# Holding a queue of loads back until an early tile has landed, in a kernel that TensorE fills

## The chip, the cores and the metric

One core of one Trainium2 chip. The metric is the time of one execution in device microseconds. Executions of this kernel differ from each other by up to 2 us, so a median of several is quoted, and most of this document is about that spread.

Engine names: PE is TensorE, PEld its weight loads, DVE VectorE, ACT ScalarE, POOL GpSimd, SP SyncE, which here issues most DMAs. "L232" is line 232 of the kernel.

## The reference

Layer norm of x (2048 x 512, bf16), then the sum of x, a linear-attention block and a gated feed-forward block:

```python
xn = layernorm(x)
# A: q, k, v = xn @ wqkv, 32 heads of 16; phi(t) = (t + 1 if t > 0 else exp(t)) + 1e-6
#    kv = sum_s phi(k)^T v ; z = sum_s phi(k) ; o = phi(q) kv / (phi(q) z + 1e-6) ; A = o @ wo
# B: (silu(xn @ w_gate) * (xn @ w_up)) @ w_down,   w_gate, w_up: 512 x 1792
out = x + A(xn) + B(xn)
```

## The kernel before

x is cut into 16 tiles of 128 rows (128 KB each, x0 to x15). For each tile VectorE makes the statistics (`bn1`, `bn2`), ScalarE the reciprocal deviation (`rs`), VectorE the scaled tile (`lna_dve`), TensorE transposes it (tiles 0 to 3) and projects it to K (`kproj`). `phi` of a K tile ends in a VectorE operation that writes `pk` and so frees the PSUM bank. The first Q projection (`qproj(0)`) needs the bank that the first K tile used, so it waits for that operation.

All engines run their own lists in the order in which they are written. The loads, in issue order on each queue:

```python
K.add("act", lambda e: e.preload_act_table_set("natural_log_exp_and_others"))
for h, eng in ((0, "sp"), (1, "act")):
    load(eng, ("x", 0, h), ...)        # x0 in two halves
xload("sp", 1)
xload("sp", 2)
wload("act", 1, 0, 2)                  # K weights, first half, 256 KB
xload("sp", 3)
wload("act", 1, 1, 2)                  # K weights, second half
wload("sp", 0)                         # Q weights, 512 KB
xload("act", 4)
xload("act", 5)
for t in range(6, 16):
    xload("sp", t)
```

The start of the program, which is the order that counts on VectorE:

```python
bn1(0); bn2(0); rs(0); bn1(1); lna_dve(0); transp(0, 0); keep_busy(NFILL, 256)
bn2(1); rs(1); evac(0, 0)
bn1(2); bn2(2); rs(2); lna_dve(1); transp(1, 1); evac(1, 1)
bn1(3); bn2(3); rs(3)                  # <- VectorE needs x3 here
k0 = kproj(0)
lna_dve(2); transp(2, 2); evac(2, 2, "dve")
k1 = kproj(1, late=True)
lna_dve(3); transp(3, 3); evac(3, 3)
k1 = k1()
norm(4)                                # <- bn1(4): x4
k2 = kproj(2); k3 = kproj(3)
stat(5)                                # <- bn1(5): x5, and only then:
k0()                                   # pk of tile 0, frees the bank
q0 = qproj(0)                          # the first Q matmul
# ... (cut) ...
```

`keep_busy(NFILL, 256)` issues filler matmuls on constants so that TensorE does not fall idle; NFILL is 3.

## Time and profile before

| | before |
|---|---|
| time, median of the first 3 runs | 216.06 us |
| time of the profiled execution | 216.84 us |
| its span | 215.1 us |
| PE busy | 209.6 us (97%) |
| first Q matmul in it | 12.37 us |
| x3 landed in it | 7.30 us |

From the page of the kernel before, the span and the first line of busy time and share:

```profile
span 215.1 us, 2648 instructions
PE 209.6 (97%) x996; PEld 96.7 (45%) x1015; DVE 102.1 (47%) x178; ACT 67.0 (31%) x132; POOL 41.3 (19%) x79
```

TensorE is the limit, so only time in which it stands idle can be won. The chain of waits, followed back from the end, tells where that is. These are its pieces in order of time; the columns are start in us, length in us, and what it was:

```profile
2.18 5.12 DMA x_sb<-in_A_x_dram
7.30 0.02 issue
7.32 0.70 DVE stats L232
8.05 0.18 DVE mv L235
8.23 0.31 DVE xn L245
...
10.94 0.59 DVE stats L232
...
11.74 0.59 DVE pk L295
12.32 0.05 issue
12.37 1.04 PE pb L312 x4
```

A load of x (x3, by its place) holds VectorE to 7.32. From there VectorE's list runs to `pk` and that releases the first Q matmul at 12.37. After that the pieces of the chain are PE, but for "issue" pieces of 0.05 us or less and VectorE's last output of 0.42 us. VectorE's own timeline shows the wait in brackets (start, length, engine, line, operation, operands, idle time before it and what ended it):

```profile
5.89 0.38 DVE L245 TENSOR_SCALAR xn<-x_sb,mv,rstd 128x512 bf16<-128x512 bf16 x1
7.32 0.69 DVE L232 BATCH_NORM_STATS2 stats<-x_sb 128x6 f32<-128x512 bf16 x1 [1.05 <-DMA x_sb<-in_A_x_dram]
```

Each load counts up its semaphore once for each of the 16 DMA engines. Of x3's sixteen counts fifteen had come by 6.16 us and the last came at 7.30 us.

### The profile page before, as it was taken

To read this page: it belongs to the slowest core of one execution; us is meant where nothing else is said; L and a number is where in the kernel's file an instruction comes from. 1 tells how busy PE (TensorE), PEld (TensorE's weight loads), DVE (VectorE), ACT (ScalarE), POOL (GpSimd) and SP (SyncE) were. 2 spreads that over 40 slices of the span, in tenths; PEclk is the share of its full clock that TensorE was granted. 3 is DMA by queue.
4 is the path that set the end of the run, shared out by engine and by line. 5 is a ranking of instruction groups with operands and counts; after the bars stand their busy time and mean duration, and the time that the engine had idled before them with its cause. 6 is when DMAs were issued, how large, how long until landed. Compare 5 with 4: busy or idle time off the path is not lost.

```text
span 215.1 us, 2648 instructions
## 1 busy us (share of the span) xinstructions
PE 209.6 (97%) x996; PEld 96.7 (45%) x1015; DVE 102.1 (47%) x178; ACT 67.0 (31%) x132; POOL 41.3 (19%) x79
## 2 busy tenths in 40 slices
PE   8799999999999999999999999999999999999995
PEld 3344444444544444444444444444444444444454
DVE  4699797556977633373433533222234423222121
ACT  3575665447363333321001333021123322110000
POOL 4164898999301100000000000000000000000000
PEclk9999999999999999999999999999999999999999
DMA  6923236999200399400000000000000000000001
GB/s 194 346 71 74 50 75 181 317 369 356 74 0 3 84 230 338 128 3 24 0 24 24 27 0 0 2 24 27 24 24 0 0 3 24 26 24 18 30 27 49
DMA packets 21725, 17.74 MB, mean 82 GB/s; under 512 B 7376, under 2 KB 21712, under 8 KB 21712
## 3 DMA queue, kind: packets, MB, share of 16 engines
q1 hardware_dynamic: 20736, 16.72, 26.1%
q10 hardware_dynamic: 976, 0.85, 1.3%
q8 instruction: 8, 0.13, 0.3%
q14 instruction: 5, 0.04, 0.1%
HBM read 11.80 MB, written 4.19 MB: 74 GB/s over the span
## 4 chain that ended last, share of the span: by engine, by line
PE 93%; DMA 2%; DVE 2%; issue 1%; SPq 1%
PE pb L444 45%; PE pb L547 22%; PE pb L312 6%; PE pb L543 6%; PE pb L319 6%; PE pb L301 5%; DMA x_sb<-in_A_x_dram 2%; DVE stats L232 1%; SPq L160 1%; PE pb L469 0%; PE pb L509 0%; DVE xn L245 0%; PE pb L494 0%; DVE pk L295 0%; DVE mv L235 0%
## 5 line engine op out<-in xcount | busy, mean ns | idle before, releaser
L452 ACT ACTIVATE sil<-pb 128x512 bf16<-128x512 f32 x56 | 33.3, 597 | 101.4 <-PE pb L444 100.2
L457 DVE TENSOR_TENSOR hT<-pb,sil 128x512 bf16<-128x512 f32 x56 | 38.5, 689 | 47.0 <-PE pb L444 46.3
L444 PE MATMUL pb<-xnT,wg 128*128 128x512 bf16 x217 | 57.0, 379 | 0.4
L444 PE MATMUL pb<-xnT,wu 128*128 128x512 bf16 x221 | 57.2, 379 | 0.1
L547 PE MATMUL pb<-wd,hT 128*128 128x512 bf16 (+1 forms) x234 | 50.9, 366 | 0.2
L547 PEld LDWEIGHTS pb<-wd,hT 128*128 128x128 bf16 x238 | 23.3, 98 | 25.1
L553 DVE TENSOR_TENSOR out_sb<-pb,x_sb 128x512 bf16<-128x512 f32 (+1 forms) x17 | 11.2, 660 | 47.2 <-PE pb L547 47.2
L444 PEld LDWEIGHTS pb<-xnT,wu 128*128 128x128 bf16 x224 | 21.9, 98 | 26.0
L444 PEld LDWEIGHTS pb<-xnT,wg 128*128 128x128 bf16 x224 | 21.7, 98 | 25.8 <-issue 0.4
L291 ACT ACTIVATE ef<-pb 128x512 bf16<-128x512 f32 x32 | 18.8, 593 | 10.9 <-PE pb L301 5.5
L292 POOL TENSOR_SCALAR ef<-ef 128x512 bf16<-128x512 bf16 x32 | 19.5, 616 | 11.9 <-ACT ef L291 11.5
L543 PE MATMUL pb<-M,pqT 128*128 128x512 bf16 (+1 forms) x67 | 16.5, 366 | 0.1
L301 PE MATMUL pb<-wqkv,xnT 128*128 128x512 bf16 x64 | 16.3, 379 | 0.0
L312 PE MATMUL pb<-xnT,wqkv 128*128 128x512 bf16 x63 | 16.1, 379 | 0.1
L319 PE MATMUL pb<-pk,xn 128*128 128x512 bf16 x61 | 15.9, 379 | 0.2
L295 DVE SCALAR_TENSOR_TENSOR pk<-pb,ef 128x512 bf16<-128x512 f32 x16 | 10.9, 686 | 6.1 <-POOL ef L292 5.6
L232 DVE BATCH_NORM_STATS2 stats<-x_sb 128x6 f32<-128x512 bf16 x16 | 10.9, 682 | 4.2 <-DMA x_sb<-in_A_x_dram 4.2
L295 DVE SCALAR_TENSOR_TENSOR pqT<-pb,ef 128x512 bf16<-128x512 f32 x16 | 11.0, 687 | 3.5 <-POOL ef L292 3.4
L543 PEld LDWEIGHTS pb<-M,pqT 128*128 128x128 bf16 x68 | 6.6, 98 | 7.4 <-DVE pqT L538 0.3
L312 PEld LDWEIGHTS pb<-xnT,wqkv 128*128 128x128 bf16 x64 | 6.2, 98 | 7.9 <-DVE pk L295 0.8
L319 PEld LDWEIGHTS pb<-pk,xn 128*128 128x128 bf16 x64 | 6.3, 98 | 7.5
L332 POOL TENSOR_TENSOR zacc<-zacc,pk 128x512 f32<-128x512 f32 x8 | 9.2, 1155 | 0.2
(52 smaller groups left out, 77.4 us busy)
## 6 DMA issues: line engine op xcount, KB each, us to landing
rscr<-rden SPq DMA_DIRECT2D x4, 512.0 KB, 6.3
pk<-rscr SPq DMA_DIRECT2D x4, 512.0 KB, 5.3
out_dram<-out_sb SPq DMA_DIRECT2D x15, 128.0 KB, 1.7
wg<-in_B_w_gate_dram SPq DMA_DIRECT2D x2, 896.0 KB, 6.4
wu<-in_B_w_up_dram SPq DMA_DIRECT2D x2, 896.0 KB, 7.8
wd<-in_B_w_down_dram SPq DMA_DIRECT2D x2, 896.0 KB, 13.5
x_sb<-in_A_x_dram SPq DMA_DIRECT2D x13, 128.0 KB, 5.0
wqkv<-in_A_wqkv_dram SPq DMA_DIRECT2D x2, 512.0 KB, 6.0
```

The costliest lines, as they stand in the source:

```text
L232: K.add("dve", lambda e: e.bn_stats(stats[:, t, :], x_sb[:, t, :]), r=xk(t), w=[("st", t)])
L291: K.add("act", lambda e: e.activation(buf, banks[b][:, :], ACT.Exp), r=[B(b)], w=[bkey])
L292: K.add("pool", lambda e: e.tensor_scalar(out=buf, in0=buf, scalar1=1.0 + 1e-6, scalar2=0.0, op0=ALU.min, op1=ALU.max), r=[bkey], w=[bkey])
L295: return lambda: K.add("dve", lambda e: e.scalar_tensor_tensor(out=dst, in0=banks[b][:, :], scalar=1e-6, in1=buf, op0=ALU.max, op1=ALU.add ...
L301: K.add("pe", [(lambda e, c=c: e.matmul(banks[b][:, :], xnT[:, c, t * P:(t + 1) * P], wqkv[:, c, D:2 * D], start=(c == 0), stop=(c == NDC ...
L312: K.add("pe", [(lambda e, c=c: e.matmul(banks[b][:, :], wqkv[:, c, g * P:(g + 1) * P], xnT[:, c, C * 512:(C + 1) * 512], start=(c == 0), s ...
L319: K.add("pe", [(lambda e, c=c: e.matmul(banks[c][:, :], xn[:, t, c * P:(c + 1) * P], pk[:, t, :], start=(t == 0), stop=(t == NT - 1))) for ...
L444: fns.append(lambda e, c=c, b=b, w_=w_: e.matmul(banks[b][:, :], w_[:, c, fc * P:(fc + 1) * P], xnT[:, c, C * 512:(C + 1) * 512], start=(c ...
L452: K.add("act", lambda e: e.activation(sil[:, j % 2, :], banks[gb(j)][:, :], ACT.Silu), r=[B(gb(j))], w=[("sil", j % 2)])
L457: K.add("dve", lambda e: e.tensor_tensor(out=hT[:, C % 2, fc, :], in0=banks[gb(j) + 1][:, :], in1=sil[:, j % 2, :], op=ALU.mult), r=[B(gb( ...
L543: fns = [(lambda e, g=g: e.matmul(banks[bank][:, 0:hi - lo], pqT[:, g, t * P:(t + 1) * P], M[:, g, lo:hi], start=(g == 0), stop=False)) fo ...
L547: fns = [(lambda e, fc=fc: e.matmul(banks[bank][:, 0:hi - lo], hT[:, C % 2, fc, jj * P:(jj + 1) * P], wd[:, fc, lo:hi], start=False, stop= ...
```

## The change

Its intent: keep the Q weights and the later x tiles out of the DMA engines while x0 to x3 and the K weights come in, so that x3 lands earlier. SyncE waits until x2 has landed, then issues x4, the Q weights, and x5 to x15. ScalarE's queue is left with the K weights. One filler matmul fewer.

```diff
-NFILL = 3
+NFILL = 2
@@
         xload("sp", 1)
+        wload("act", 1, 0, 2)
         xload("sp", 2)
-        wload("act", 1, 0, 2)
+        wload("act", 1, 1, 2)
         xload("sp", 3)
-        wload("act", 1, 1, 2)
+        K.add("sp", [], r=[("x", 2)])
+        xload("sp", 4)
         wload("sp", 0)
-        xload("act", 4)
-        xload("act", 5)
-        for t in range(6, 16):
+        for t in range(5, 16):
             xload("sp", t)
```

The lines of the K weights move only in the text; on each queue their place is the same. Two things change on the queues besides the wait: x4 and x5 leave ScalarE's queue, and the Q weights now stand ahead of x5. On VectorE, GpSimd and ScalarE (its two DMA issues aside) no instruction moves.

## The prediction

> **What bounds the kernel now.** The page gives TensorE (PE) 209.6 us busy of a 215.1 us span. The chain of waits shows PE unbroken from 12.37 us to the end, so the change can only gain before that. There the chain runs: issue of x tile 3, its DMA (2.18 to 7.30 us), its batch-norm statistics at 7.32 on VectorE, scale of tile 2, transpose (8.59), copy, scale of tile 3 (to 10.13), statistics of tiles 4 and 5, the first pk (11.65), the first Q matmul (12.37). VectorE executes in order, so its 1.05 us wait for x3 (timeline) delays all of it.
>
> **Why x3 is late.** Landing records in the trace: x0 3.1, x1 3.66, first half of the K weights 4.55, x2 5.04, second half 6.41, x3 7.30, x4 7.47, Q weights 9.33, x5 9.38, x15 12.89 us. Windows of 2 us show the DMA engines full (share 1.00 to 1.09) from 2 to 10 us, at 286 to 378 GB/s. Fifteen of x3's sixteen completions had come by 6.16 us; one engine was 1.1 us later. The Trainium skill, "DMA: Bandwidth & Descriptors", section "Issuing engines are not separate DMA queues", says that transfers of all issuing engines run on the same 16 DMA engines and interleave; this trace agrees: x4, from ScalarE's queue, takes turns with x3.
>
> **What the change does.** No bytes and no work are added. Only x0 to x3 and the K weights (1.0 MB) are issued at first; at about 310 GB/s from 2.0 us they are through at 5.4. With a late engine I estimate x3 landed at 5.6 to 6.3. SyncE waits for x2 (5.04), then issues x4, Q, x5 to x15 at 0.45 to 0.57 us apiece. The DMA engines run dry for about 1 us near 6. Estimates: x4 lands at 7.4 (as before), Q 9.0, x5 9.5, x15 13.2: each before or close to its use.
>
> **The new chain.** Statistics of x3 start when VectorE has scaled tile 1, at 6.27 (1.05 earlier). The transpose of tile 2 is held by the first K projection until about 7.65 (0.94 earlier). Scale of tile 3 took 0.77 us beside the GpSimd minimum at 9.37; other scales take 0.38, so some 0.2 may come back. Statistics of tile 5 start about 9.7, close to x5's landing. First Q matmul about 11.3: gain 1.1 us. PE stays full afterwards, so the end moves by the same.
>
> **Fillers.** One 256-column filler is about 0.21 us, within 5.49 to 6.13. The next transposes wait for xn until 6.33, so nothing is gained on the chain. "TensorE: Matmul & The Clock Gate", Part 1, describes a clock that activity releases; the trace agrees: four transposes take 0.61 and 0.59 us before 6.76, 0.40 after. I expect no later release.
>
> **Prediction:** 215.0 us, range 214.5 to 215.8; faster by over 2% 0.01, within 2% 0.98, slower by over 2% 0.01.
>
> **Right if:** the statistics' wait for DMA near 7 us is under 0.2; x3 lands by 6.3; the first Q matmul is at 11.0 to 11.6; afterwards PE has no new waits; transposes near 6.3 take 0.6 and later ones 0.4.
>
> **Wrong if:** a late DMA engine still holds x3 past 6.5; x5, now behind Q, lands past 10 and stops VectorE; SyncE's issuing, ending near 12 instead of 8.9 us, delays the DMA transposes enough to reach the K projection of tile 4; or the clock is released a window later, costing 1 us or more.

## More of the kernel before

When I write "slow execution" below, I mean one whose x tile came late. It has nothing to do with a lowered clock.

The busy times by stretch of 1 us say how loaded the DMA engines are. The last two columns are their share and what they moved in GB/s:

```profile
5.00:6.00 1.00, 1.00 (x8) 0.71 (x7) 0.97 (x5) 0.76 (x3) 0.00 (x0) 1.00 1.00 309
6.00:7.00 1.00, 1.00 (x8) 0.56 (x7) 0.27 (x1) 0.77 (x4) 0.00 (x0) 1.00 0.95 306
7.00:8.00 1.00, 0.78 (x4) 0.16 (x2) 0.68 (x1) 0.55 (x1) 0.00 (x0) 1.00 1.06 347
```

They are full: shares of 0.95 to 1.06.

## The result

| | before | changed |
|---|---|---|
| median of 6 runs | 216.11 us | 216.41 us |
| lowest to highest | 216.04 to 217.1 | 216.07 to 216.59 |
| profiled execution | 216.84 | 216.59 |
| its span | 215.13 | 214.75 |
| x3 landed | 7.30 | 6.33 |
| x5 landed | 9.38 | 10.42 |
| first Q matmul | 12.37 | 11.99 |

The ratio of the changed kernel to the one before is 1.0001, with a 95% interval of 0.9981 to 1.0021: the same. (A ratio is the mean time of one kernel's fast runs over that of the other's fast runs of the same rounds, so it is not quite the ratio of the medians.) The predicted 215.0 us, range 214.5 to 215.8, was too fast: 1.4 us below the median.

Note the trap. The two profiles taken alone show a gain of 0.38 us, in the span and in the first Q matmul. The medians show none.

The chain of waits of the changed kernel, in order of time, columns as before:

```profile
1.71 3.61 DMA x_sb<-in_A_x_dram
5.32 0.02 issue
5.34 0.33 SPq L160
5.67 0.04 issue
5.71 0.44 SPq L160
6.14 0.04 issue
6.19 4.24 DMA x_sb<-in_A_x_dram
10.42 0.02 issue
10.45 0.70 DVE stats L232
...
11.36 0.59 DVE pk L295
11.94 0.05 issue
11.99 1.04 PE pb L312 x4
```

The chain is a new one. x2 lands (5.32), SyncE wakes and issues x4, the Q weights and x5, and VectorE waits for **x5** until 10.45. Its timeline shows both ends. The wait for x3 is gone (6.47, no bracket) and one of 0.71 us for x5 has come:

```profile
6.47 0.69 DVE L232 BATCH_NORM_STATS2 stats<-x_sb 128x6 f32<-128x512 bf16 x1
...
9.55 0.18 DVE L235 BATCH_NORM_AGGREGATE mv<-stats 128x2 f32<-128x6 f32 x1
10.45 0.69 DVE L232 BATCH_NORM_STATS2 stats<-x_sb 128x6 f32<-128x512 bf16 x1 [0.71 <-DMA x_sb<-in_A_x_dram]
```

TensorE's timeline shows what it costs there:

```profile
11.99 1.04 PE L312 MATMUL pb<-xnT,wqkv 128*128 128x512 bf16 x4 [0.90 <-DVE pk L295]
```

And the stretches of 1 us show the DMA engines run dry and move 141 and 152 GB/s after the pause, where they moved 306 and 347 before:

```profile
5.00:6.00 1.00, 0.62 (x6) 0.34 (x6) 0.79 (x3) 0.80 (x3) 0.00 (x0) 1.00 0.49 169
6.00:7.00 1.00, 0.39 (x5) 0.34 (x6) 0.96 (x4) 0.68 (x3) 0.00 (x0) 1.00 0.63 141
7.00:8.00 1.00, 1.00 (x10) 0.47 (x8) 0.64 (x3) 0.92 (x4) 0.00 (x0) 1.00 0.63 152
```

The means hide two dips. In slices of 0.2 us of the same trace the rate is 0 GB/s at 6.0 us, 276 at 6.4 (this is x4), 36 at 7.0 and 317 at 7.8. So the engines take up x4 at nearly the old rate and then almost stop again before the Q weights flow. Why they do so was not tested.

### The profile page after: what moved, and what is told of

The parts are those of the page before. It is cut to its first block, busy times and chain, and to the rows that moved or that the text cites. A ratio compares the mean times of both kernels' runs of the same rounds, so it can differ in the third digit from the quotient of the medians.

```text
span 214.8 us, 2665 instructions
## 1 busy us (share of the span) xinstructions
PE 209.0 (97%) x1014; PEld 96.0 (45%) x1014; DVE 101.8 (47%) x178; ACT 66.9 (31%) x132; POOL 41.4 (19%) x79
## 4 chain that ended last, share of the span: by engine, by line
PE 93%; DMA 4%; DVE 1%; SPq 1%; issue 0%
PE pb L444 45%; PE pb L547 23%; PE pb L312 7%; PE pb L543 6%; PE pb L319 6%; PE pb L301 5%; DMA x_sb<-in_A_x_dram 4%; SPq L160 1%; PE pb L509 0%; PE pb L494 0%; PE pb L469 0%; DVE stats L232 0%; DVE pk L295 0%; DVE out_sb L553 0%; PE pb L485 0%
## 5 line engine op out<-in xcount | busy, mean ns | idle before, releaser
L444 PE MATMUL pb<-xnT,wg 128*128 128x512 bf16 x224 | 57.8, 379 | 0.0
L444 PE MATMUL pb<-xnT,wu 128*128 128x512 bf16 x224 | 57.8, 379 | 0.0
L292 POOL TENSOR_SCALAR ef<-ef 128x512 bf16<-128x512 bf16 x32 | 19.6, 616 | 11.4 <-ACT ef L291 11.3
```

Source lines behind the costliest of these rows:

```text
L292: K.add("pool", lambda e: e.tensor_scalar(out=buf, in0=buf, scalar1=1.0 + 1e-6, scalar2=0.0, op0=ALU.min, op1=ALU.max), r=[bkey], w=[bkey])
L444: fns.append(lambda e, c=c, b=b, w_=w_: e.matmul(banks[b][:, :], w_[:, c, fc * P:(fc + 1) * P], xnT[:, c, C * 512:(C + 1) * 512], start=(c ...
```

## The experiments

The theories that the runs were to tell apart:

- **A**: the Q weights ahead of x5 make x5 late, and that gives back what x3 gained. A1 and A2 split it: is it the pause in the loads, or the order?
- **B**: the profile that I predicted from was a slow execution. Usually x3 lands on time in the kernel before too, and there is less to win.
- **C**: the filler that was taken away costs as much as the queues gain.
- **D**: the wait for x2 is what keeps a late DMA engine away from x3.

Four kernels ran on one chip at first. "x3" and "x5" below are landing times in the profiled execution, and "first Q" the start of the first Q matmul in it, all read from the trace.

### before_again: the kernel before, unchanged

No edit.

> The kernel before, unchanged, to see how much one execution differs from another. Theory A (the new place of the Q weights, ahead of x5, holds VectorE at x5 and gives back what x3 gained): nothing is claimed of this run beyond its median, 216.1 us. Theory B (the profile of before that I read was an unusually slow execution, 216.84 us against a median of 216.1, with one late DMA engine at x3): here x tile 3 lands by 6.7 us instead of 7.30, the first Q matmul is at 11.5 to 11.8 instead of 12.37, and the profiled span is near 214.4 instead of 215.1. If x3 lands after 7.1 and the first Q matmul is after 12.2 again, B is wrong.

Measured: median 216.06 us, six runs from 215.57 to 217.20; the eleven runs of the same kernel beside it, 215.34 to 217.07, median 215.79. The profiled execution was the slowest of the six, 217.20 us, with x3 at 7.50 and the first Q matmul at 12.57. B's number for this profile missed. But the same kernel on the same chip ran up to 1.9 us faster at other times (215.34), so one profile could not settle it. The looks below do.

### fillers_only: two fillers, the old queues

```diff
-NFILL = 3
+NFILL = 2
```

> The kernel before with two fillers instead of three, the queues untouched. Theory C (one filler fewer lets the TensorE clock be released later and costs what the queues gain): about 0.5 to 1.0 us slower than before, 216.6 to 217.1, with transposes of 0.6 us after 6.8 in its profile. Theories A and B: nothing, 216.1 within 0.3.

Measured: median 215.72 us (215.68 to 215.81), ratio to before 0.9987, interval 0.9961 to 1.0012. Theory C, which asked for 216.6 or more, falls. The profile is the first one of the old queues with x3 on time: x3 at 6.21, first Q at 11.17, 215.68 us.

### queue_only: the new queues, three fillers

```diff
-NFILL = 2      # against the changed kernel
+NFILL = 3
```

> The changed queues with three fillers as before. Theory C: 0.5 to 1.0 us faster than before, 215.1 to 215.6. Theories A and B: as the changed kernel, 216.1 to 216.6, with VectorE waiting 0.5 to 1.0 us for x5 near 10 us, and the first Q matmul near 12.0.

Measured: median 216.06 us (215.86 to 216.63), ratio to before 1.0004, interval 0.9977 to 1.0031. x3 at 5.99, x5 at 9.70, VectorE waited 0.41 us for x5 (a little under the 0.5 expected), first Q at 11.27 (expected near 12.0). The median is 0.27 us above that of before on the same chip, where C asked for 0.5 to 1.0 below. It is just under the 216.1 to 216.6 of A and B; the changed kernel itself was not on this chip. The filler plays no part that these runs can see; an effect below about 0.3 us is not excluded (the interval of fillers_only ends at 1.0012).

### x5_before_q: x5 ahead of the Q weights, the wait kept

```diff
         xload("sp", 4)
+        xload("sp", 5)
         wload("sp", 0)
-        for t in range(5, 16):
+        for t in range(6, 16):
```

> The changed kernel with x5 issued ahead of the Q weights, behind the same wait for x2. Theory A: the 0.71 us wait of the statistics of x5 goes, the first Q matmul is at 11.2 to 11.4 instead of 11.99, and the time is 0.6 to 0.8 us below the changed kernel, 215.6 to 215.8, unless Q itself, landing some 0.3 us later at 10.4, becomes late (it is needed at 11.2). If A is wrong and the first Q matmul is held by something else (TensorE's own K projections end at 11.1): no change, 216.4.

Measured: median 215.67 us (215.50 to 216.97), x5 at 7.44, no wait for it, Q weights at 10.00, first Q at 10.91. As A expects, and even earlier. The changed kernel itself was not on this chip, so it was repeated beside it.

### after_again and x5_before_q_again: both on one chip

No new edit.

> The changed kernel again, on the chip of the three runs that follow. Theory A (Q ahead of x5 gives the gain back): VectorE waits 0.4 to 0.8 us for x5, x5 lands at 9.7 to 10.5, the first Q matmul is at 11.3 to 12.0, and the median is 0.3 to 0.5 us above the kernel with x5 ahead of Q. If the first Q matmul is below 11.2 with no wait for x5, A does not describe the usual execution.

> The changed kernel with x5 ahead of the Q weights, as before on another chip. Theory A: no wait for x5, first Q matmul at 10.9 to 11.2, x3 landed by 6.4, median 0.3 to 0.5 us below the changed kernel of these rounds. If the earlier profile was luck: median equal to the changed kernel within 0.15 us.

Measured: the changed kernel 216.33 us (215.85 to 216.74), with x5 ahead of Q 215.69 us (215.58 to 216.06), before 216.17 us (215.80 to 217.37). The changed kernel's profile fell on its fastest run: x5 at 9.68, a wait of 0.38 (0.4 was the lower edge), first Q at 11.25. With x5 ahead of Q: no wait, first Q at 11.01. The medians differ by 0.64 us, more than the 0.3 to 0.5 written down. Its ratio to before is 0.9976, interval 0.9953 to 0.9999.

### no_wait: the changed kernel without the wait

```diff
         xload("sp", 3)
-        K.add("sp", [], r=[("x", 2)])
         xload("sp", 4)
```

> The changed kernel without the wait for x2, the order of the queue kept (x4, Q, x5 on). Theory A1 (x5 is late because the wait lets the DMA engines run dry for over 1 us, and the order is harmless): x5 lands at 8.6 to 9.2, VectorE does not wait for it, first Q matmul at 10.9 to 11.2 when x3 is on time. Theory A2 (the order alone makes x5 late): x5 lands after 9.8 and VectorE waits. Theory D (the wait is what keeps one late DMA engine away from x3): here, as in the kernel before, some executions have x3 after 7 and the run times spread by over 1 us; if x3 is on time and the times spread by under 0.5 us, D is not supported.

Measured: median 216.37 us (215.50 to 216.61). x5 landed at 9.47, between the two expectations. VectorE did not wait for it, but only because this execution had x2 late (5.78; VectorE waited 0.57 us for it), so everything after was later: first Q at 11.61. In an execution on time VectorE comes to x5 at about 9.4 (9.38 and 9.40 in the looks below, 9.37 in the next run), so 9.47 would just about do. By this one profile the order alone leaves x5 no slack, and the pause adds 0.2 to 1.0 us to it (9.68 to 10.51 with the pause). So the wait takes both: with the pause kept, the other order removes it (x5_before_q), and without the pause it would be near nothing by this estimate. The times spread by 1.1 us, as D expected; but the changed kernel, with the wait, spread by 0.89 us in the same rounds, and x3 at 6.81 was not past 7, so this run says little about D.

### x5_first_no_wait: x5 ahead of Q, and no wait

Both edits above at once.

> No wait for x2, and x4 and x5 on the sync queue ahead of the Q weights; ScalarE's queue holds the K weights alone. All data early: x3 by 6.3, x5 by 7.5, Q by 9.2 us. Theory A: first Q matmul at 10.9 to 11.2, median 0.3 to 0.5 us below the changed kernel. Theory D: slow executions of 0.8 us or more above the fastest come back, as in the kernel before, since Q is in flight behind x3; without D, the times spread by under 0.5 us and this is the best of the four.

Measured: median 216.08 us (215.49 to 216.92). In the profile, the fastest run, all data came early: x3 6.03, x5 6.79, Q weights 8.29, first Q at 10.88. But two of six runs were over 216.3, so this was not the best of the four in the median, where the kernel with the wait was. That is what D expects.

### before_look1, before_look2, before_look3: three more profiles of the kernel before

No edit.

> The kernel before, for one more profile. Theory B (the profile I predicted from was a slow execution, and x3's landing makes the difference): if x3 lands by 6.4 us the first Q matmul is at 10.8 to 11.5 and the time is under 216.2; if x3 lands later, the first Q matmul comes 5.0 to 5.2 us after it (7.30 to 12.37 and 7.50 to 12.57 in the two profiles so far). In either case the span is the first Q matmul plus 202.7 to 203.0. Without B: x3 after 7.1 and the first Q matmul near 12.4 in all three looks.

> As the first look: theory B expects x3 by 6.4 and the first Q matmul at 10.8 to 11.5, or a late x3 and the first Q matmul 5.0 to 5.2 us after it; without B, x3 after 7.1 again.

> As the first look. Of the three looks, theory B expects at least one with x3 by 6.4 and the first Q matmul below 11.5.

Measured, with the two earlier profiles of the same kernel:

| execution of the kernel before | time | x3 landed | first Q | span | span less first Q |
|---|---|---|---|---|---|
| the profile predicted from | 216.84 | 7.30 | 12.37 | 215.13 | 202.76 |
| before_again | 217.20 | 7.50 | 12.57 | 215.48 | 202.91 |
| before_look1 | 215.37 | 6.13 | 10.89 | 213.65 | 202.76 |
| before_look2 | 216.84 | 7.29 | 12.36 | 215.12 | 202.76 |
| before_look3 | 215.40 | 6.20 | 10.92 | 213.68 | 202.76 |

B holds for the profile that I predicted from: it was a slow execution. The five profiles fall into two groups, 1.4 us apart or more, and the landing of x3 tells which. The rest of the program takes 202.76 us from the first Q matmul on in four of the five. When x3 is late, the first Q matmul follows 5.07 us after it in all three. VectorE's timeline of the first look, at the place of the 1.05 us wait, has no wait at all:

```profile
5.91 0.38 DVE L245 TENSOR_SCALAR xn<-x_sb,mv,rstd 128x512 bf16<-128x512 bf16 x1
6.21 0.69 DVE L232 BATCH_NORM_STATS2 stats<-x_sb 128x6 f32<-128x512 bf16 x1
```

And the chain of waits of that look has no load in it. It runs through TensorE's warm-up and VectorE's work to the same place:

```profile
0.84 4.42 PE pb L222 x10
...
6.75 0.86 PE pb L301 x4
...
9.46 0.59 DVE stats L232
...
10.26 0.59 DVE pk L295
10.84 0.05 issue
10.89 1.04 PE pb L312 x4
```

So in a good execution of the kernel before there was no wait at x3 to take away, and the change can only add one at x5.

Two things in these profiles I had overlooked. First, x3 is not all of the difference. The first Q matmul is 1.48 us earlier in before_look1 than in the profile predicted from: 1.11 us because the statistics of x3 start earlier (6.21 against 7.32), and 0.37 because the scaling of tile 3 on VectorE takes 0.40 us and not 0.77. In the three late executions that scaling starts within 0.01 us of GpSimd's minimum, as here in the first profile:

```profile
9.36 0.77 DVE L245 TENSOR_SCALAR xn<-x_sb,mv,rstd 128x512 bf16<-128x512 bf16 x1
9.37 0.61 POOL L292 TENSOR_SCALAR ef<-ef 128x512 bf16<-128x512 bf16 x1 [5.95 <-ACT ef L291]
```

In before_look1 VectorE starts 0.13 us ahead (8.24 against 8.37), and then the scaling takes 0.40 us and GpSimd's minimum 0.74. No run was made to test this pair.

Second, the two groups are not the whole picture. Of the 45 runs of the kernel before, 33 lie between the groups, at 215.48 to 216.68 us, and the median of 216.06 is among them. No profile of this kernel fell there, so what the usual run waits for was not seen. A late x2 is a candidate: no_wait above and hold_q_only below had x2 at 5.78 and 5.74, no wait at x3, and a first Q matmul at 11.61 and 11.57.

### x5_after_x8: the suspected wait made larger

```diff
         wload("sp", 0)
-        for t in range(5, 16):
+        for t in (6, 7, 8, 5) + tuple(range(9, 16)):
```

> The changed kernel with x5 put behind x6, x7 and x8 in the sync queue: the suspected wait made larger. Theory A: x5 lands about 1.1 us later than in the changed kernel (10.8 to 11.5), VectorE waits 1.4 to 2.0 us for it, the first Q matmul comes 1.5 to 1.6 us after x5's landing (12.3 to 13.0), and the time is 0.9 to 1.3 us above the changed kernel's 216.4, so 217.2 to 217.7. If VectorE's wait at x5 were off the chain that decides: no change.

Measured: x5 at 11.33, a wait of 1.65 us, first Q at 12.90, which is 1.57 us after x5; median of four runs 217.30 us (217.06 to 218.14), ratio to before 1.006 (1.0024 to 1.0096). All of these are in their ranges. The changed kernel was not in these rounds. The profiled execution was the slowest, 218.14 us: beyond x5 it lost 0.65 us after the first Q matmul, 0.49 of it in a wait of TensorE for a DMA transpose at 44.65 us and 0.16 in a stall at 67.11. VectorE's timeline:

```profile
9.53 0.18 DVE L235 BATCH_NORM_AGGREGATE mv<-stats 128x2 f32<-128x6 f32 x1
11.36 0.69 DVE L232 BATCH_NORM_STATS2 stats<-x_sb 128x6 f32<-128x512 bf16 x1 [1.65 <-DMA x_sb<-in_A_x_dram]
```

x5's landing decides when the first Q matmul starts with the new queue, almost microsecond for microsecond: 0.91 us later in x5, 0.91 in the first Q matmul (10.42 to 11.33 and 11.99 to 12.90, against the changed kernel's first profile).

### The last four: after_third, hold_q_only, x5_before_q_third, x5_first_no_wait_again

hold_q_only is the kernel before with one line added:

```diff
         wload("act", 1, 1, 2)
+        K.add("sp", [], r=[("x", 2)])
         wload("sp", 0)
         xload("act", 4)
```

> The changed kernel a third time, beside the next three. Theory A: VectorE waits 0.3 to 0.8 us for x5, first Q matmul 11.2 to 12.0, median 215.9 to 216.5, spread under 1 us. x3 by 6.4 (theory D).

> The kernel before with only the wait for x2 added ahead of the Q weights; x4 and x5 stay on ScalarE's queue, three fillers. Theory D (traffic of the sync queue behind x3 is what a late engine comes with): x3 by 6.4, x5 by 8.5, no wait of VectorE at either, Q at about 8.8, first Q matmul at 10.9 to 11.2, median 215.4 to 215.8 with no run over 216.5. Rival (x4 and x5 beside x3 are what matters, or it is chance): x3 after 7 in some executions and runs over 216.5 in about one of three, as in the kernel before.

> The changed kernel with x5 ahead of Q, a third time. Theories A and D: median 215.4 to 215.8, 0.3 to 0.6 us below the changed kernel of these rounds, first Q matmul 10.9 to 11.2, at most one of six runs over 216.5.

> The same order without the wait, again. Theory D: slow executions as in the kernel before, so two or more of six runs over 216.3, and a median 0.2 us or more above the kernel with the wait. If the wait does nothing: median within 0.15 us of the kernel with the wait and the same spread.

Measured, on one chip (that of the looks), with before at 216.00 us (215.28 to 216.81):

| kernel | median of 6 | lowest to highest | x3 | x5 | wait for x5 | first Q |
|---|---|---|---|---|---|---|
| after_third | 216.56 | 215.82 to 217.57 | 6.19 | 10.51 | 0.64 | 12.08 |
| hold_q_only | 215.79 | 215.48 to 216.05 | 6.50 | 7.16 | 0 | 11.57 |
| x5_before_q_third | 215.73 | 215.28 to 215.87 | 6.04 | 7.92 | 0 | 11.16 |
| x5_first_no_wait_again | 215.97 | 215.64 to 217.62 | 6.17 | 6.89 | 0 | 11.29 |

x5 ahead of Q is 0.83 us below the changed kernel here, more than the 0.3 to 0.6 expected. The changed kernel missed its edges narrowly (median 216.56 for 216.5, first Q 12.08 for 12.0), and its spread, 1.75 us, was wider than expected. hold_q_only missed several of its numbers: its profiled execution had x2 late, at 5.74, and VectorE waited 0.68 us for it. Its times met theirs, none over 216.05. The no-wait order again has two of six runs over 216.3 and a median 0.24 us above the same order with the wait. But one of the two, 217.62 us, had a granted clock of 0.992, where every other run has 0.999 or 1.0. I estimate that at 1.7 us (0.008 of 214 us), so it is no evidence for D; without it the difference of the medians is 0.15 us, which the expectation gives to a wait that does nothing. First Q at 11.29 with no late tile is again the scaling of tile 3: 0.81 us, 0.04 us ahead of GpSimd's minimum. VectorE's timeline of x5_before_q_third at x5 (one line lower in this kernel) for comparison with 10.45 in the changed kernel:

```profile
9.55 0.18 DVE L236 BATCH_NORM_AGGREGATE mv<-stats 128x2 f32<-128x6 f32 x1
9.65 0.66 DVE L233 BATCH_NORM_STATS2 stats<-x_sb 128x6 f32<-128x512 bf16 x1
```

### All runs of each kernel together

| kernel | runs | median | lowest to highest | runs over 216.5 |
|---|---|---|---|---|
| before | 45 | 216.06 | 215.28 to 217.37 | 9 |
| changed | 18 | 216.44 | 215.82 to 217.57 | 6 |
| x5 ahead of Q, with the wait | 18 | 215.70 | 215.28 to 216.97 | 1 |
| x5 ahead of Q, no wait | 12 | 216.08 | 215.49 to 217.62 | 2 |

These are the four kernels that ran most. The runs come from several chips, so small differences of the medians are not to be pressed. The median of the kernel with x5 ahead of Q is below those of before and of the changed kernel wherever it ran beside them. It is not shown to be the best of what ran: on its own chip fillers_only is within 0.05 us of it (215.72 to 215.67), and hold_q_only within 0.06 (215.79 to 215.73). Against before its three ratios are 0.9997, 0.9976 and 0.9987, and only the second interval (0.9953 to 0.9999) leaves out 1. It is a gain of 0.03 to 0.24%.

On D: in the nine profiles of kernels with the wait, x3 landed between 5.93 and 6.50. In the nine without it, three times after 7.2 and once at 6.81. With the wait and x5 early (x5_before_q three times and hold_q_only), 1 of 24 runs was over 216.5. Without the wait (before, fillers_only, no_wait and x5_first_no_wait twice), 14 of 69 (13 of 68 without the run of lowered clock; none of the six of fillers_only, which has the old queues). This agrees with D, but the counts are small and x2 was late with the wait as well (5.49 and 5.74). D is not shown, and chance is not ruled out. What makes one of the sixteen engines late in one execution and not in the next stays open.

## Why the prediction was wrong

**The bound, right.** Only what comes before the first Q matmul counts. The span is that moment plus 202.76 us in four of the five profiles of before and in the first changed one. It is not quite so in all: it is 203.13 in no_wait and 203.41 in x5_after_x8, where TensorE waited 0.19 and 0.49 us for a DMA transpose after 43 us.

**The mechanism at x3, right, and smaller than written.** x3 landed at 6.33, 5.93 and 6.19 in the three profiles of the changed kernel (5.6 to 6.3 predicted; the first is a hair over), and VectorE's wait for it was gone in all. The scaling of tile 3 came back to 0.41 us in the first of them, 0.36 less, where I had guessed 0.2.

**The step that failed first: "so the end moves by the same", subtracted from the median.** The gain of 1.1 us was read from an execution of 216.84 us and taken off a median of 216.06. The three late executions of before have x3 at 7.3 to 7.5; the two on time have no wait for x3 and a first Q matmul at 10.9, already 0.4 us earlier than the 11.3 that I predicted for the changed kernel. A sum from the numbers of the profile alone would have been 216.84 less 1.1, that is 215.7, and not 215.0. In terms of the chain: a median of 216.06, less the 1.72 us between time and span in before_look1, less 202.76, is by estimate a first Q matmul at about 11.6, not 12.37. About 0.8 of the 1.1 us was not there in the median run, though no profile of such a run exists.

**The term that was mis-sized second: "x5 9.5".** It landed at 10.42, 9.68 and 10.51, and 9.70 in queue_only. The Q weights, 9.0 in the prediction, came at 10.10, 9.31 and 10.18. My estimates let the DMA engines go straight back to full rate after the pause; they moved 141 and 152 GB/s in the two stretches that followed. VectorE came to x5 at 9.73, 9.33, 9.90 and 9.31 and waited 0.71, 0.38, 0.64 and 0.41 us. Counted from the landing of x2, on which both depend, VectorE came to x5 after 4.4 us in all four and x5 landed after 4.8 to 5.1; the prediction has 4.7 and 4.5. I had named this risk ("x5, now behind Q, lands past 10 and stops VectorE") and given it no weight in the sum. x5_before_q takes that wait away and is 0.64 and 0.83 us faster in the medians of the same rounds; x5_after_x8 makes it 0.94 us larger and its median is 0.89 us above the changed kernel's 216.41, though in other rounds.

The two terms together, 0.8 and 0.4 to 0.7, cover the 1.4 us between 215.0 and 216.41.

**Fillers, right in the time.** fillers_only is 0.9987 of before. What I said of the clock's timing was not: transposes at 5.10 already took 0.40 us in the changed kernel's profile, where I expected 0.6. The recorded release of the clock lies between 3.5 and 6.8 us in the executions that recorded one. The Trainium skill, "TensorE: Matmul & The Clock Gate", Part 1, says that the window is free-running and the release run-variable. These runs agree with the second; no run here shows the first. An earlier release did not bring an earlier first Q matmul: 10.89 with a release at 6.36 (before_look1), 11.16 with one at 4.15 (x5_before_q_third, where x2 cost a wait of 0.27), neither with a wait for x3 or x5. In before_look1 the chain does run through the warm-up matmuls, so there an earlier release might have helped; this was not tested.

**SyncE's later issuing, rightly harmless.** It ended at 11.45 instead of 8.86, and the K projection of tile 4 started at 17.18, not late. x15 landed at 14.19 (13.2 predicted) and nothing waited for it.

**The page on the queues.** The Trainium skill, "DMA: Bandwidth & Descriptors", section "Issuing engines are not separate DMA queues", says that loads from all issuing engines run on the same 16 DMA engines and interleave. The trace of before agrees: in the window from 2 to 10 us both queues are at work, with 68.5% (SyncE's) and 34.5% (ScalarE's) of the 16 engines' span. So x4 and x5 on ScalarE's queue had a place in a second list, and that place let x5 land at 8.3 to 9.4 in the old queues. Moving x5 behind 512 KB of Q weights gave that place up.

## What to carry to other kernels

When a load is held back or moved, ask of every later load in that queue when its reader comes to it in the good case, not only of the load that is to gain; an in-order engine turns the first late one into the new wait. A profile is one execution: before taking its wait off a median, see whether its own time is the median, and if it is not, take another profile, since the wait may be just what made it slow. And do not count on a drained queue to resume at full rate: here it moved 141 and 152 GB/s in the two stretches after the pause.

## What the Trainium skill lacked or had wrong

- "DMA: Bandwidth & Descriptors" gives rates and latencies, and in "Latency and other measured facts" an HBM latency of 0.2 us on average and 2 us at high load. It has a row on two engines that are usually slower, but nothing on one of the sixteen falling behind in some executions only; which engine it was, the traces here do not tell. Here fifteen engines had finished x3 by 6.16 us and the last by 7.30 (6.57 and 7.50 in before_again). Most packets of 1 KB took 46 ns, single ones 0.6 to 1.4 us; that such a packet is what made the engine late is not shown. With the load that was late the first Q matmul came 1.48 us later, 1.11 of it at the load itself.
- The same page has a first-byte latency of about 0.6 us for loads issued by SyncE or ScalarE, and no figure for how a drained set of engines gets back to rate. Here x4, issued from 5.34 us on, had its first completion at 7.00 us, and the engines moved 141 and 152 GB/s in the two stretches of 1 us after the pause against 306 and 347 in the same stretches of before.
- "Perfetto Trace Analysis" does not say that the profiled execution is to be compared with the median of the runs. Here it was 216.84 us against 216.06, and the difference was as large as the gain that was looked for.
